# Pre-norm transformer block, one core: attention bursts of one key tile for four quads of heads, 512 columns wide, from the third tile on

## The chip, the cores and the metric

The kernel runs on one core of a Trainium2 chip. The metric is device time in microseconds (us) of one execution. Times come from timed executions and from one profiled execution whose trace names every instruction, its engine, its start and its length.

The engines are TensorE (PE in the profile; its weight loads are PEld), VectorE (DVE), ScalarE (ACT), GpSimd (POOL) and SyncE (SP, which here only issues transfers).

## The reference, cut to what matters

The input x has 2048 rows of 1024 columns; there are 32 heads of 32 columns that share one key head and one value head; the feed-forward part is 3584 wide. Everything is bf16.

```python
def _A_ref(x, wq, wk, wv, wo):          # attention, H = 32, Dh = 32
    q = (x @ wq) as (B, H, S, Dh)
    k = x @ wk; v = x @ wv               # one head for all
    scores = einsum("bhqd,bkd->bhqk", q, k) * Dh ** -0.5
    p = softmax(scores)
    o = einsum("bhqk,bkd->bhqd", p, v)
    return o as (B, S, H * Dh) @ wo
def _B_ref(x, w_gate, w_up, w_down):
    return (sigmoid(x @ w_gate) * (x @ w_up)) @ w_down
h = x + _A_ref(layernorm(x), ...)
out = h + _B_ref(layernorm(h), ...)
```

## The kernel before, in words

**Layout.** `QT` holds the queries transposed: 128 partitions are four heads of 32 dimensions (four strips), 8 slots make 32 heads, 2048 columns are the rows of x. `kT4` holds the transposed keys four times, once per strip. `V` holds the values as 16 key tiles of 128 keys by 32. A tile is 128 rows of x; there are 16 tiles, in 8 units of two.

**Attention.** The work is cut into 64 groups, `ORDER[g] = (t, i)`: tile `t`, and two of the eight slots (eight heads). A group has eight bursts. One burst (`s_burst`, L666 to L680) takes two key tiles: for each key tile four matmuls, one for each strip of 32 partitions, run side by side in TensorE, each 256 columns wide (two slots of 128 rows). They fill two of three pairs of banks in `S_ps`. ScalarE makes two exponentials of 128x1024 from a burst (`one_exp`, L696) and writes them into a ring `Pr` of 18 such tiles, that is, nine bursts. A burst may start when the exponentials of one and a half bursts earlier are out of the banks.

**Values and row sums.** `pv_group` (L759 on) multiplies a group's 16 tiles of exponentials with `V`: four matmuls side by side, one for each strip of 32 output partitions, 256 columns each (L798). For the row sums, VectorE adds the tiles of a group (`add_pair`: L737 adds the two key tiles of a burst, L746 merges the results) into `pairs`, and TensorE multiplies what is left with ones (L777, one or two sets of four matmuls a group, a plan says which) into the right half of the same bank. Groups 0 to 2, group 8 and the very last burst use ones on every tile instead (L795). The bank is evacuated by VectorE: a copy (L816), a 32x32 transposition of the sums (L817), later a reciprocal (L822), a transposition back (L824) and a product (L828) that writes the result over the queries in `QT`.

**Everything else on TensorE.** The projections, wo (both L333), gate and up (L1010) and down (L1080) are groups of full 128x128 matmuls. They and the values share the two banks of `X_ps`; a bank opens again when its evacuation is done.

**Feed-forward part.** A unit's gate and up weights come in "halves" of 256 columns (512 KB, one transfer on SP's queue, L242) into slots that become free: `wgu`, parts of `QT`, and late ones in `Pr` and others. When only the first tile of a unit is ready, `first_tile` runs a pair of halves with 128 columns for that tile alone; the second tile follows as a "later" step. Either the four halves are held for it in their slots, or they are loaded a second time; `may_hold` decides. Down uses 28 matmuls of 512 columns for half a tile.

**Order of the work.** One Python loop writes the order when the kernel is built. It keeps a clock for each engine and issues a burst as soon as its banks should be free, otherwise a piece of the values' group or of the next other group; `dve_fill` puts VectorE's additions into its gaps. The string `PV_PLAN` has a letter for each group that says how its values are started, and a capital says that its sums end in one set of matmuls. On the chip every engine runs its list in this order, held only by semaphores.

Of the kernel before, what the change touches and what calls it, by code (L numbers as in the profile page):

```python
# [7 lines left out]
BF16 = mybir.dt.bfloat16  # L8
# [4 lines left out]
P = 128  # L13
# [71 lines left out]
def bass_sequential_preLN__grouped_kv_mqa__glu_gated_glu__prompt_kernel(  # L85
# [39 lines left out]
    HEAD = ['uuL', 'V', '', '', 'LVLu', 'UU', 'PP', 'LWL', 'zu', 'PPL', 'VV', 'uLPLz', 'PPVL', 'U', 'UPL', 'Pz', 'U', 'UP', 'PzP', 'VV', 'PPU']  # L125
    HEAD_U = [5, 6, 4, 7]
# [12 lines left out]
    with ExitStack() as es:  # L139
        EC = es.enter_context  # L140

        def sb(name, shape, dt=BF16):
            return EC(nc.sbuf_tensor(name, [P] + shape, dt))
# [15 lines left out]
        l8 = sb("l8", [QC // 32], F32)  # L159
# [4 lines left out]
        rs = sb("rs", [2 * NT], F32)  # L164
        vz = sb("vz", [2 * NT])
        sd = sb("sd", [2 * NT])
        powers = sb("powers", [4])
# [70 lines left out]
        def _(unused):  # L238
# [299 lines left out]
            def wq_need(q):  # L538
                return wq_val[q // 2]

            def q_rows(g):
                t, i = ORDER[g]
                return QT[:, 2 * i:2 * i + 2, t * P:(t + 1) * P]

            def q_ready(g):
                t, i = ORDER[g]
                return [q_val[(0, (t, i))]] if t < TPQ else [q_val[(t // TPQ, 2 * i)], q_val[(t // TPQ, 2 * i + 1)]]

            def vq_group(p, qs, on_act=False):
# [70 lines left out]
                return burst(k)[0] * NQ + burst(k)[1]  # L620

            def summed(g):
                return g >= G_SUM and g not in NO_SUM
# [41 lines left out]
            def s_burst(k):  # L665
                g, b = quad(k), burst(k)[2]  # L666
                t, i = ORDER[g]
                mode("s")
                need(pe, (c_e, 2 * k - 1) if k > 0 else None, k_val[b], *q_ready(g), *(xnT_ready(0, 1) if k < 2 else ()))
                for kt in range(2):  # L670
                    for j in range(4):
                        bank = ((2 * k + j // 2) % 3) * 2 + j % 2
                        ins = pe.matmul(S_ps[:, bank, kt * QC:(kt + 1) * QC],  # L673
                                        lhsT=kT4[DH * j:DH * (j + 1), (2 * b + kt) * P:(2 * b + kt + 1) * P],
                                        rhs=QT[DH * j:DH * (j + 1), 2 * i:2 * i + 2, t * P:(t + 1) * P],
                                        start=True, stop=True, tile_position=(DH * j, 0))
                        if kt == 1 and j % 2 == 1:
                            c_s.inc(ins, 0.115, 0.3)
# [42 lines left out]
            def homes(g):  # L721
                return {7: HOME[g % 2][6]} if one_sum(g) else HOME[g % 2]

            def add_pair(k):
                g, b = quad(k), burst(k)[2]
                t, slot, home = (2 * ring(k) + 2) % RP, SLOT[g % 2][b], homes(g)
# [25 lines left out]
                for i, (x, y) in enumerate(steps):  # L752
                    put("p", T_ADD, lambda i=i: merge(i), lambda x=x, y=y: max(when(slot_use[x]), when(slot_use[y])))
# [2 lines left out]
            ot_val = {}  # L756
            ols_read = {}

            def pv_group(g):  # L759
                c = UNIT[ORDER[g][0]]  # L760
                items = []
                is_sum = summed(g)
# [50 lines left out]
                def evac(bank, tick):  # L813
# [5 lines left out]

                    def recip():  # L820
                        need(dve, free)
                        r_ = c_dve.inc(dve.reciprocal(l8[:], ols[:, QC:2 * QC].rearrange("p (a b) -> p a b", b=32)[:, :, 0]), 0.23)  # L822
                        need(dve, r_)
                        t_[0] = c_dve.inc(dve.transpose(ols[:, QC:2 * QC], l8[:].unsqueeze(2).to_broadcast([P, QC // 32, 32])), 0.4)  # L824

                    def mult():
                        need(dve, t_[0])
# [519 lines left out]
            since_s = [0.0]  # L1347
            idle = 0
            while True:
                if wo_val[0] is None and pv_done[0] >= 2 * BPG:  # L1350
                    need(pool, (c_pv, 2 * BPG))
                    wo_val[0] = dma(pool, wo[:], A_wo.rearrange("(q p) n -> p q n", p=P), d_wo, 2048)
# [2 lines left out]
                act_run(k_pe[0])  # L1355
                kk = k[0]
                end = pv_next[0] == NQC * NQ - 1
                pv_ready = pv_next[0] < NQC * NQ and kk >= min(BPG * (pv_next[0] + 1) + 1, NB - end)
                due = when((c_e, 2 * kk - 1))
                plan = PV_PLAN[min(pv_next[0], NQC * NQ - 1)].lower()  # L1360
                late = plan in "ce" and kk == BPG * (pv_next[0] + 1) + 1 and not busy(pv[0])
# [78 lines left out]
                if (pv_next[0] < NQC * NQ and kk > BPG * pv_next[0] + 1 and blocked()  # L1440
                        and UNITS[ffn_list[0][1]][-1] not in hnT_val):
                    pv[0] = pv_group(pv_next[0])
                    pv_next[0] += 1
                    continue
# [37 lines left out]
```

## Time and profile before

| what | us |
|---|---|
| median of 3 timed runs | 1103.26 (1101.07 to 1103.36) |
| the profiled execution | 1102.48 |
| its span, first to last instruction | 1100.7 |
| PE busy | 1075.6, 98% of the span, 15,088 matmuls in the trace |
| PEld busy (weight loads) | 672.5, 61% |
| ACT busy | 1009.7, 92% |
| DVE busy | 885.8, 80% |
| mean DMA rate over the span | 144 GB/s |
| granted TensorE clock, mean | 0.997 |

Busy time is the union of the instructions' lengths. Matmuls overlap with the next one's start, so the pace of TensorE is read from the starts in a timeline, not from their lengths. In the profile, "out<-in" names the tiles an instruction writes and reads, and "<-" behind idle time names what ended it.

### The profile page before, as it was taken

How to read it: one execution, taken by the hardware profiler on the slowest of the kernel's cores; microseconds unless marked ns; L12 is line 12 of the kernel's file. 1: busy time of each engine (PE TensorE's matmuls, PEld its weight loads, DVE VectorE, ACT ScalarE, POOL GpSimd, SP SyncE). 2: the span in 40 equal slices, each digit the busy share in tenths (PEclk: the TensorE clock that was granted, in tenths of full speed). 3: DMA queues.
4: the chain of work that ended last, by engine and by line, in shares of the span. 5: the costliest groups of instructions: out<-in, count | busy, mean ns of one | idle time of the engine just before them, and what ended most of it. 6: DMA issues, size and time to landing. Idle time of an engine off the chain costs nothing. (4 is left out here: it accounts for less than half of the span.)

```text
span 1100.7 us, 34688 instructions
## 1 busy us (share of the span) xinstructions
PE 1075.6 (98%) x15088; PEld 672.5 (61%) x15148; DVE 885.8 (80%) x1586; ACT 1009.7 (92%) x1155; POOL 67.1 (6%) x136
## 2 busy tenths in 40 slices
PE   7999999999999999999999999999999999999999
PEld 5553467654776457664676547764676547764884
DVE  7759968888888888888889888898988888888311
ACT  6999999999999999999999999999999999999110
POOL 4500110100000000000000000000000000000000
PEclk9899999999999999999999999999999999999999
DMA  9852328760675318660585619771495609771760
GB/s 220 141 137 86 106 69 231 223 176 23 158 212 150 91 30 231 174 164 26 153 223 153 145 42 249 197 193 35 120 245 156 153 26 239 201 199 50 163 159 20
DMA packets 299000, 158.88 MB, mean 144 GB/s; under 512 B 39008, under 2 KB 293216, under 8 KB 298848
## 3 DMA queue, kind: packets, MB, share of 16 engines
q1 hardware_dynamic: 293040, 146.43, 51.7%
q0 software_dynamic: 2544, 9.44, 2.6%
q8 instruction: 119, 1.95, 0.8%
q10 hardware_dynamic: 3264, 0.79, 0.4%
q14 instruction: 33, 0.27, 0.1%
HBM read 144.57 MB, written 4.19 MB: 135 GB/s over the span
## 5 line engine op out<-in xcount | busy, mean ns | idle before, releaser
L696 ACT ACTIVATE Pr<-S_ps 128x1024 bf16<-128x1024 f32 x992 | 939.7, 1127 | 4.2 <-PE S_ps L673 3.2
L737 DVE TENSOR_TENSOR pairs<-Pr 128x1024 bf16<-128x1024 bf16 x479 | 324.0, 683 | 51.5 <-ACT Pr L696 48.8
L746 DVE TENSOR_TENSOR pairs<-pairs 128x1024 bf16<-128x1024 bf16 x407 | 280.4, 689 | 25.7 <-DVE pairs L737 1.4
L1010 PE MATMUL X_ps<-QT,wgu 128*128 128x256 bf16 (+1 forms) x2528 | 264.2, 253 | 1.9 <-DMA wgu<-in_B_w_up_dram 1.3
L1010 PEld LDWEIGHTS X_ps<-QT,wgu 128*128 128x128 bf16 x2528 | 198.9, 98 | 51.1 <-issue 30.2
L1080 PE MATMUL X_ps<-zone,hact 128*128 128x512 bf16 (+2 forms) x880 | 206.5, 373 | 6.1 <-issue 5.7
L673 PE MATMUL S_ps<-QT,kT 32*128 32x256 bf16 x4096 | 204.1, 273 | 7.2 <-ACT Pr L696 1.9
L1010 PE MATMUL X_ps<-QT 128*128 128x256 bf16 (+1 forms) x1712 | 172.6, 249 | 0.4 <-DVE ols L817 0.4
L673 PEld LDWEIGHTS S_ps<-QT,kT 32*128 32x128 bf16 x4096 | 61.0, 92 | 151.5 <-ACT Pr L696 128.0
L1010 PEld LDWEIGHTS X_ps<-QT 128*128 128x128 bf16 x1712 | 130.7, 98 | 27.7 <-issue 17.1
L1080 PEld LDWEIGHTS X_ps<-zone,hact 128*128 128x128 bf16 x924 | 79.0, 98 | 99.4 <-issue 24.9
L798 PE MATMUL X_ps<-Pr,V 128*32 128x256 bf16 x3968 | 129.7, 273 | 0.4
L1031 ACT ACTIVATE gu<-X_ps 128x512 f32<-128x512 f32 x112 | 80.4, 718 | 47.5 <-PE X_ps L1010 47.5
L1052 DVE SCALAR_TENSOR_TENSOR hact<-gu,X_ps 128x512 bf16<-128x512 f32 x112 | 76.4, 682 | 47.4 <-PE X_ps L1010 46.9
L798 PEld LDWEIGHTS X_ps<-Pr,V 128*32 128x32 bf16 x3968 | 98.2, 96 | 20.4 <-issue 9.3
L333 PE MATMUL X_ps<-zone 128*128 128x512 bf16 (+3 forms) x576 | 78.7, 281 | 2.7 <-ACT QT L591 1.3
L333 PE MATMUL X_ps<-wo,QT 128*128 128x512 bf16 x240 | 60.6, 380 | 1.6 <-issue 1.1
L333 PEld LDWEIGHTS X_ps<-zone 128*128 128x128 bf16 x576 | 39.5, 100 | 31.9 <-issue 12.9
L348 POOL CAST mean<-mv 128x1 f32<-128x1 bf16 x28 | 8.3, 298 | 818.1 <-DVE mv L923 804.8
L816 DVE COPY ols<-X_ps 128x256 f32<-128x256 f32 x64 | 27.0, 421 | 22.8 <-PE X_ps L777 20.0
L333 PEld LDWEIGHTS X_ps<-wo,QT 128*128 128x128 bf16 x256 | 22.5, 97 | 29.0 <-issue 7.4
L1090 DVE SCALAR_TENSOR_TENSOR hx<-X_ps,hx 128x512 bf16<-128x512 f32 (+2 forms) x33 | 22.1, 670 | 21.7 <-PE X_ps L1080 21.5
(79 smaller groups left out, 449.6 us busy)
## 6 DMA issues: line engine op xcount, KB each, us to landing
wgu<-in_B_w_gate_dram SPq DMA_DIRECT2D x68, 512.0 KB, 5.0
wgu<-in_B_w_up_dram SPq DMA_DIRECT2D x68, 512.0 KB, 5.3
QT<-in_B_w_gate_dram SPq DMA_DIRECT2D x45, 512.0 KB, 5.5
QT<-in_B_w_up_dram SPq DMA_DIRECT2D x45, 512.0 KB, 5.3
zone<-in_B_w_down_dram POOLq DMA_DIRECT2D x14, 512.0 KB, 5.3
out_dram<-hx SPq DMA_DIRECT2D x31, 128.0 KB, 1.7
hx<-in_A_x_dram SPq DMA_DIRECT2D x15, 256.0 KB, 3.2
Pr<-in_B_w_gate_dram SPq DMA_DIRECT2D x5, 512.0 KB, 7.2
```

The source lines that it names most:

```text
L333: ins = pe.matmul(sel(bank), lhsT=a, rhs=b, start=(i == 0), stop=(i == last))
L673: ins = pe.matmul(S_ps[:, bank, kt * QC:(kt + 1) * QC], lhsT=kT4[DH * j:DH * (j + 1), (2 * b + kt) * P:(2 * b + kt + 1) * P], rhs=QT[DH * ...
L696: c_e.inc(act.activation(out=p_tile(k, n % 2), in_=S_ps[:, 2 * pr:2 * pr + 2, :].rearrange("p a (b q) -> p (a b) q", q=QC), func=ACTF.Exp, ...
L737: add_half[k] = slot_use[slot] = c_dve.inc(dve.tensor_tensor(out=pairs[:, slot, :].rearrange("p (j q) -> p j q", j=4), in0=p4[:, :, 0, :], ...
L746: slot_use[x] = slot_use[y] = c_dve.inc(dve.tensor_tensor(out=pairs[:, x, :], in0=pairs[:, x, :], in1=pairs[:, y, :], op=ALU.add), T_ADD, ...
L798: ins = pe.matmul(bank[DH * j:DH * (j + 1), 0:QC], lhsT=V[:, 2 * b + kt, :], rhs=rhs(j), start=first and is_sum, stop=last and plain, tile ...
L816: dve.tensor_copy(out=ols[:, 0:QC], in_=bank[:, 0:QC])
L1010: ins = pe.matmul(bank[:, j * m:(j + 1) * m], lhsT=halves[i][:, dt, j % 2 * P:(j % 2 + 1) * P], rhs=QT[:, dt, r0:r0 + m], start=(dt == 0), ...
L1031: tanh_val[n] = c_act.inc(act.activation(out=slot, in_=bank, func=ACTF.Tanh, scale=0.5), T_TANH, 0.1)
L1052: gu_read[n] = c_dve.inc(dve.scalar_tensor_tensor(out=hact[:, 2 * fs[0]:2 * fs[0] + ft, r0:r0 + len(ts) * P], in0=slot.rearrange("p (a b) ...
L1080: ins = pe.matmul(bank[:, 0:n], lhsT=hact[:, ft, tt * P:(tt + 1) * P], rhs=wd[:, ft, c0:c0 + n], start=(ft == 0), stop=(ft == NFT - 1))
L1090: v = c_dve.inc(dve.scalar_tensor_tensor(out=hv, in0=bank[:, 0:n], scalar=0.5, in1=hv, op0=ALU.mult, op1=ALU.add), 0.03 + n * 0.00113, 0.08)
```

## The change

From group 8 on (the third tile), `wide(g)` holds. Two neighbouring groups of a tile become one block of four slots (16 heads): the first group takes key tiles 0 to 7 of the block, the second key tiles 8 to 15. A burst is one key tile: four matmuls side by side, each 512 columns wide (four slots of 128 rows). It still fills four banks and feeds two exponentials of 128x1024. The values are four matmuls of 512 columns a burst, so that the group fills a whole bank; the first group's bank is copied to a new buffer `olp`, the second's is added to it. The row sums have their own group (`sum_group`) in a bank of its own, once for each block, which the loop starts some bursts after the values (`pv_follow`). VectorE adds the tiles of two neighbouring bursts and merges them into two running tiles for the block. The division is done once a block, on 512 columns.

Beside that, `HR` (tiles of x and h kept) is 4 instead of 5, the two constants `powers` lie in spare columns of `nmean`, `PV_PLAN` is another string, group 8 sums by addition as the others do, the last two bursts use ones directly, and `may_hold` lets units 1 to 3 hold no weights, so that their split steps load them again.

```diff
-    HR = 5
+    HR = 4
-    PV_PLAN = "aadbAdcadEEAEAAAaEEACEAcaEEAECAEaEEECEAAaEEAEEAAaEEAEEAAaEEEeEAa"
+    PV_PLAN = "aaaaAeAaaeaaaeaAaebabaaAdaddaaaAdababaaadabadaaCdabadaaEcaaaacaa"
-    G_SUM, NPB, NO_SUM = 3, 4, (NQ,)
+    G_SUM, NPB = 3, 4
-        ols = sb("ols", [2 * QC], F32)
+        ols = sb("ols", [512], F32)
+        olp = sb("olp", [512], F32)
...
+            def wide(g):
+                return g >= NQ
+            def key_tile(g, b):
+                return ORDER[g][1] % 2 * BPG + b
...
             def direct(k):
-                return k == NB - 1
+                return k >= NB - 2
...
+                if wide(g):
+                    kt = key_tile(g, b)
+                    for j in range(4):
+                        ins = pe.matmul(S_ps[:, ((2 * k + j // 2) % 3) * 2 + j % 2, :],
+                                        lhsT=kT4[DH * j:DH * (j + 1), kt * P:(kt + 1) * P],
+                                        rhs=QT[DH * j:DH * (j + 1), i // 2 * 4:i // 2 * 4 + 4, t * P:(t + 1) * P],
+                                        start=True, stop=True, tile_position=(DH * j, 0))
+                        if j % 2 == 1:
+                            c_s.inc(ins, 0.109, 0.3)
+                    return
...
+            def add_wide(k):
+                g, b = quad(k), burst(k)[2]
+                if b % 2 == 0:
+                    return
...
+                def run(hh):
+                    x = take()
+                    need(dve, (c_e, 2 * k + hh + 1), slot_use[x])
+                    slot_use[x] = c_dve.inc(dve.tensor_tensor(out=dst(x), in0=p_tile(k - 1, hh), in1=p_tile(k, hh), op=ALU.add),
+                                            T_ADD, 0.08)
...
+                def merge(hh):
+                    x, y = run_slot[hh], run_slot[2 + hh]
+                    need(dve, slot_use[x], slot_use[y])
+                    slot_use[x] = slot_use[y] = c_dve.inc(dve.tensor_tensor(
+                        out=pairs[:, x, :], in0=pairs[:, x, :], in1=pairs[:, y, :], op=ALU.add), T_ADD, 0.08)
+                    spare.append(y)
...
+            def pv_wide(g):
...
+                        for j in range(4):
+                            ins = pe.matmul(bank[DH * j:DH * (j + 1), :], lhsT=V[:, kt, :],
+                                            rhs=p_tile(k, j // 2)[:, j % 2 * 2:j % 2 * 2 + 2, :],
+                                            start=b == 0, stop=b == BPG - 1, tile_position=(0, DH * j), skip_group_check=True)
...
+                def evac(bank, tick):
+                    if x % 2 == 0:
+                        force("a", lambda: g - 1 in ols_read)
+                        need(dve, tick, ols_read[g - 1])
+                        olp_val[0] = c_dve.inc(dve.tensor_copy(out=olp[:], in_=bank), 0.62, 0.08)
+                        return olp_val[0]
+                    need(dve, tick, olp_val[0])
+                    olp_val[0] = c_dve.inc(dve.tensor_tensor(out=olp[:], in0=bank, in1=olp[:], op=ALU.add), 0.62, 0.08)
+                    pv_follow[0] = sum_group(g)
+                    return olp_val[0]
...
+            def sum_group(g):
...
+                    for j in range(4):
+                        ins = pe.matmul(bank[DH * j:DH * (j + 1), :], lhsT=ones[:],
+                                        rhs=pairs[:, sum_wide[(g, j // 2)], j % 2 * 512:(j % 2 + 1) * 512],
+                                        start=True, stop=not final, tile_position=(0, DH * j), skip_group_check=True)
...
+                    free = c_dve.inc(dve.transpose(ols[:], bank), 0.75, 0.08)
+                        r_ = c_dve.inc(dve.reciprocal(l8[:], ols[:].rearrange("p (a b) -> p a b", b=32)[:, :, 0]), 0.23)
+                        t_[0] = c_dve.inc(dve.transpose(ols[:], l8[:].unsqueeze(2).to_broadcast([P, 512 // 32, 32])), 0.75)
+                        v = c_dve.inc(dve.tensor_tensor(out=q_rows(g), in0=olp[:].rearrange("p (a b) -> p a b", a=4),
+                                                        in1=ols[:].rearrange("p (a b) -> p a b", a=4), op=ALU.mult), 0.7)
...
-                return c == NU - 1 or n == 0 and c > 0 or c == 0 and n < 2 or 4 * n + 8 <= 4 + c
+                return c == NU - 1 or c == 0 and n < 2 or 4 * n + 8 <= 4 + c
...
+                if not busy(pv[0]) and pv_follow[0] is not None and (
+                        not busy(cur[0]) and not ffn_list or min(bank_time(b) for b in range(2)) <= k_pe[0] + 0.05 and (
+                            PV_PLAN[pv_next[0] - 1].isupper() or k[0] >= NB or
+                            pe_mode[0] == "s" and busy(cur[0]) and cur[0].left() > 0.9 or
+                            k[0] >= BPG * pv_next[0] + 5)):
+                    pv[0], pv_follow[0] = pv_follow[0], None
```

Counted in the two built programs, instruction by instruction (sets are four matmuls side by side):

| on the engines' lists | before | after |
|---|---|---|
| score bursts of 8 matmuls, 256 columns | 512 | 64 |
| score bursts of 4 matmuls, 512 columns | 0 | 448 |
| value sets of 256 / of 512 columns | 1024 / 0 | 128 / 448 |
| ones sets of 256 / of 512 columns | 138 / 0 | 56 / 30 |
| gate and up matmuls of 256 / of 128 columns | 2624 / 1920 | 2368 / 2432 |
| other full matmuls | the same | the same |
| changes between score, value or ones, and full matmuls | 1090 | 1147 |
| VectorE additions of 128x1024 | 886 | 908 |
| VectorE evacuation and division chains of 256 / 512 columns | 64 / 0 | 8 / 28 (and 28 copies) |
| exponentials of 128x1024; tanh | 1024; 112 | 1024; 112 |
| halves of gate and up weights loaded | 240 | 268 |

More of the change, by code (lines that the diff above doesn't have):

```diff
@@ L546, in q_ready @@
                 t, i = ORDER[g]
+                if wide(g):
+                    return [q_val[(t // TPQ, i // 2 * 4 + x)] for x in range(4)]
                 return [q_val[(0, (t, i))]] if t < TPQ else [q_val[(t // TPQ, 2 * i)], q_val[(t // TPQ, 2 * i + 1)]]
@@ L622, in summed @@
             def summed(g):
-                return g >= G_SUM and g not in NO_SUM
+                return g >= G_SUM
             def direct(k):
-                return k == NB - 1
+                return k >= NB - 2
             def burst_no(g, b):
@@ L722, in homes, with unheld, take, dst @@
                 return {7: HOME[g % 2][6]} if one_sum(g) else HOME[g % 2]
+            run_slot, sum_wide, spare = {}, {}, []
+            def unheld():
+                return [x for x in spare if slot_use[x] != "held"]
+            def take():
+                x = min(unheld(), key=lambda x: when(slot_use[x]))
+                spare.remove(x)
+                return x
+            def add_wide(k):
+                g, b = quad(k), burst(k)[2]
+                if b % 2 == 0:
+                    return
+                first, last = key_tile(g, b) == 1, key_tile(g, b) == KT - 1 or direct(k + 2)
+                def dst(x):
+                    return pairs[:, x, :].rearrange("p (a b) -> p a b", b=QC)
+                def run(hh):
[3 more added lines that the diff above has]
+                                            T_ADD, 0.08)
+                    if hh == 1:
+                        add_half[k - 1] = add_half[k] = slot_use[x]
+                    if first:
+                        run_slot[hh] = x
+                    else:
+                        run_slot[2 + hh] = x
+                def merge(hh):
[4 more added lines that the diff above has]
+                    spare.append(y)
+                    if last:
+                        sum_wide[(g, hh)] = x
+                for hh in range(2):
+                    put("p", T_ADD, lambda hh=hh: run(hh), lambda hh=hh: None if not unheld() else
+                        max(when((c_e, 2 * k + hh + 1)), min(when(slot_use[x]) for x in unheld())))
+                    if not first:
+                        put("p", T_ADD, lambda hh=hh: merge(hh), lambda hh=hh: when(slot_use[run_slot[2 + hh]]))
@@ L724, in add_pair @@
             def add_pair(k):
                 g, b = quad(k), burst(k)[2]
+                if wide(g):
+                    if not spare and not run_slot:
+                        spare.extend(range(NPB))
+                    add_wide(k)
+                    return
                 t, slot, home = (2 * ring(k) + 2) % RP, SLOT[g % 2][b], homes(g)
@@ L1357, in _ @@
                 end = pv_next[0] == NQC * NQ - 1
-                pv_ready = pv_next[0] < NQC * NQ and kk >= min(BPG * (pv_next[0] + 1) + 1, NB - end)
+                pv_ready = pv_follow[0] is None and pv_next[0] < NQC * NQ and kk >= min(BPG * (pv_next[0] + 1) + 1, NB - end)
                 due = when((c_e, 2 * kk - 1))
                 plan = PV_PLAN[min(pv_next[0], NQC * NQ - 1)].lower()
-                late = plan in "ce" and kk == BPG * (pv_next[0] + 1) + 1 and not busy(pv[0])
+                late = plan in "ce" and kk == BPG * (pv_next[0] + 1) + 1 and not busy(pv[0]) and pv_follow[0] is None
                 can_s = kk < NB and pv_done[0] >= ring_need(kk - 1 if late else kk)
```

77 lines of the change are left out of this document (71 added, 6 removed).

## The prediction

> **What bounds the kernel now.** I read the busy times first (the page's first part), then the windows of the steady stages, then who waits for whom on TensorE, then a timeline for the pace.
>
> ```profile
> PE 1075.6 (98%) x15088; PEld 672.5 (61%) x15148; DVE 885.8 (80%) x1586; ACT 1009.7 (92%) x1155; POOL 67.1 (6%) x136
> ```
>
> TensorE is nearly full, ScalarE close behind. The windows (length, then busy time of PE, PEld, DVE, ACT, POOL, then clock, DMA share and GB/s) show whether one share hides several stages.
>
> ```profile
> 742.00:867.00 125.00, 123.81 (x1782) 77.00 (x1783) 108.97 (x192) 125.00 (x144) 3.77 (x7) 1.00 0.59 154
> 867.00:991.00 124.00, 122.79 (x1769) 76.84 (x1775) 107.56 (x189) 123.91 (x143) 3.60 (x7) 1.00 0.58 153
> ...
> 1016.00:1101.00 85.00, 82.41 (x835) 62.93 (x836) 18.74 (x33) 8.36 (x14) 1.29 (x3) 1.00 0.49 115
> ```
>
> A unit takes some 124 us, with VectorE at 87%. After the last burst (1013) TensorE works alone for 85 us. The waits on PE's own row between 60 and 1010 us are:
>
> ```profile
> PE X_ps L1080 <- issue: 5.4, 34, 0.2
> PE X_ps L1010 <- DMA wgu<-in_B_w_up_dram: 1.3, 1, 1.3
> PE X_ps L333 <- issue: 1.1, 7, 0.2
> PE X_ps L1010 <- ACT gu L1031: 0.6, 1, 0.6
> PE S_ps L673 <- ACT Pr L696: 0.4, 1, 0.4
> PE X_ps L1010 <- DVE ols L817: 0.4, 1, 0.4
> ```
>
> Leaving "issue" aside (mostly a matmul whose record is missing), TensorE waits about 3 us in 950. So TensorE bounds the kernel: wherever ScalarE is not ready, the order has other matmuls. The time is the sum of what TensorE issues, plus its waits, and only a shorter sum makes it shorter. The pace comes from timelines (start, length, engine, line):
>
> ```profile
> 601.01 0.38 PE L1010 MATMUL X_ps<-QT 128*128 128x256 bf16 x2
> ...
> 601.32 0.40 PE L673 MATMUL S_ps<-QT,kT 32*128 32x256 bf16 x8
> 601.65 1.42 PEld L1010 LDWEIGHTS X_ps<-QT 128*128 128x128 bf16 x14 [0.21 <-issue]
> 601.65 1.70 PE L1010 MATMUL X_ps<-QT 128*128 128x256 bf16 x14
> ```
>
> ```profile
> 538.25 1.07 PE L1010 MATMUL X_ps<-QT 128*128 128x128 bf16 x16
> ```
>
> ```profile
> 1011.56 1.68 PE L1080 MATMUL X_ps<-zone,hact 128*128 128x512 bf16 x7
> ...
> 1013.50 1.71 PE L798 MATMUL X_ps<-Pr,V 128*32 128x256 bf16 x56
> ```
>
> A run's length less the last matmul's own (273, 219, 380 ns in the groups by shape), over the starts between, gives start to start: 256 columns (1.70 - 0.273) / 13 = 0.110 us; 128 columns (1.07 - 0.219) / 15 = 0.057 (most single ones 0.056); 512 columns (1.68 - 0.380) / 6 = 0.217 (most 0.216); a set of four value matmuls (1.71 - 0.28) / 13 = 0.110. Four side by side cost what one costs. A burst takes 0.33 from its start to the next work: 0.120 to the second set's start, 0.010 within it, 0.109 of streaming, and 0.09 for changing between the tiled and the full array. On the way in, the last full matmul starts at 601.01 + 0.38 - 0.273 = 601.12 and the burst 0.205 later: 0.109 streaming, 0.096 change. I take 0.093 for a change.
>
> **The change part by part,** with the counts of the two programs from the table above.
>
> (1) Scores. No trace shows four matmuls of 512 columns side by side. Ends: two sets of 256 as now (0.240 with the start offsets), or one full matmul of 512 (0.216 plus 0.010 of offsets). Sets of 256 pace like one matmul of 256, so I take the near end, 0.227. 448 bursts save 0.0135 each: -6.0 us; 0 is the other end.
>
> (2) Values. 56 groups of 16 sets at 0.1095 become 448 sets at 0.2165: -1.1 us; the ends are 0 and, should the 0.120 that some sets show go too, -2.
>
> (3) Row sums. 138 sets at 0.1095 are 15.1 us; 56 at 0.1095 and 30 at 0.2165 are 12.6: -2.5 us.
>
> (4) Split steps. 512 more matmuls of 128 columns (0.056) and 256 fewer of 256 (0.1093): +0.7 us.
>
> (5) Array changes. The sum has a place of its own, and more value groups are cut by a burst: 1147 for 1090, at 0.093: +5.3 us. This takes back most of (1).
>
> (6) VectorE. 22 more additions at 0.686 (L737 683 ns, L746 689) are +15.1 us. A chain of 256 columns costs 421 + 440 + 197 + 446 + 424 = 1928 ns; 512 columns out of PSUM cost 683 to 690 (L593, L888), 265 more than 256, and so a block of 512 with its second evacuation about 690 + 690 + 710 + 205 + 715 + 690 = 3700 against 3856 for two groups: -4 us. Net +11 us, some 1.5 a unit: 87% becomes 88 to 89%. What hides it is VectorE's idle time, 15 us a unit; if that were gone it would be paid whole. I count 0 on the path.
>
> (7) Banks. With the paces above, I laid out TensorE's work between a bank's last use and its next opening. In before the shortest is 0.86 us and 30 of them are under 1.2, and the rows above show 0.4 us of waiting for an evacuation. After, 48 are under 1.2 and two under the 0.70 that a copy or a transposition of 512 takes (0.31, 0.63). Those two lack 0.5 us; I add 0.3 for the crowd between 0.8 and 1.2: +0.8.
>
> (8) Weights. 28 more halves of 512 KB are 14.7 MB; the eight of a unit add 4.2 MB in 124 us, 34 GB/s on the 153 of the window above. SP issues each in 0.37 us and idles in between for the slots; its transposes and the output queue behind them. A half lands in a median of 5.0 to 5.5 us; the loads stand two to five bursts (4 to 10 us) ahead of their step, as in before's first unit. Bounds: 0 if all are early; 7 added steps at the 1.5 us that the one late half cost at 540.6 would be +10. I take one more late half's worth less the 1.3 of the present one: +0.4.
>
> (9) Tail and start. From the last sum to wo stand 8 down matmuls and 32 of 128 columns, 1.73 + 1.8 = 3.5 us, over a chain of 0.7 + 0.2 + 0.7 + 0.7 = 2.3: hidden. Between wo and the second tile's first use, tile 14's remaining 160 matmuls of 128 take 9.0 us, over about 7 (in before, wo ends at 1023.9 and the second tile's transpose is issued at 1027.6 and lands 3.3 later): hidden, with 2 us to spare. `HR`, `powers` and the first 41 us: the order there is the same, 0; their cover is that tile t - 4 is long written out when tile t is wanted. ScalarE issues the same list.
>
> Sum: -6.0 - 1.1 - 2.5 + 0.7 + 5.3 = -3.6 of TensorE's work, +1.2 of waits: -2.4. On the profiled 1102.48 that is 1100.1; the median of the three runs is 0.8 above the profiled one, so I give the middle, 1100.4.
>
> **The rivals.**
>
> *A, nothing measurable* (within 0.2%, 2.2 us, about what a measurement of this kernel can tell from no change). The 18 additional openings under 1.2 us and the tight weights give back 2 to 4: 1101 to 1104. For it: the waits now are 3 us in all, so they can hardly fall. Against: before's 30 such openings cost 0.4.
>
> *B, VectorE becomes the bound; slower.* The place is the evacuation behind one addition that has just begun (0.69 us): an opening with less than 0.86 + 0.69 = 1.55 us of cover then waits. After, 76 openings lack 30 us in total against that; before, 69 lack 21. It decides from about a fifth of the 30 on, 6 us; at a third it is 10 - 3.6, or 1109. Against: before paid next to nothing of its 21.
>
> *C, the second loads come late; slower.* A split step of four halves needs 7 us of transfers at the 290 GB/s of the best 10 us, and it lasts two or three bursts, 4 to 6 us. Units 3 and 6 have two or three in a row. At (8)'s upper end, 1102.5 - 3.6 + 10 = 1109. Against: the queue holds them bursts ahead.
>
> *D, more gain.* The waits go too (3 us), or the value sets lose more: 1096 to 1097.
>
> *E, the cost of a matmul is per instruction.* 3,584 score and value matmuls fewer, and if each cost but a tenth of a set of 256 (0.011), -39 us: 1063. Against: 0.110 for four side by side leaves 0.003 beyond the columns. The Trainium skill ("TensorEngine Tiling (Array Packing)", section Instruction Overhead) says that each matmul has about 60 cycles of overhead; by that, and 2.4 GHz, an estimate is 3,584 x 25 ns = 90 us, or 22 us where four overlap. The trace does not bear it out at these widths: two sets of 256 take 0.219 and one matmul of 512 takes 0.216.
>
> **How the numbers follow.** The forecast (1097.5 to 1101) 0.48; A 0.22; B 0.13; C 0.10; D 0.06; E 0.01. The range 1096 to 1108 leaves out E, and B and C beyond their middle. Faster by over 0.2%: forecast without its edge, D and E, 0.52; within: A and that edge, 0.25; slower: B and C, 0.23.
>
> **What would show it.** After: TensorE's row of waits below 6 us between 60 and 1010; a 512-column burst of 0.317 us from its start to the next work; the last burst some 2 us earlier; the stage behind it 1 to 2 us shorter; VectorE busy near 897. Wrong would be: four side by side at 512 slower than 0.24, waits on `olp`, `ols` or `pairs` on TensorE's rows (B), waits on `wgu` or `QT` transfers (C).

## The result and the profile after

| | before | after |
|---|---|---|
| median of 20 runs each, us | 1102.53 (1101.07 to 1103.83) | 1100.26 (1098.54 to 1102.60) |
| ratio, 95% interval | | 0.9978 [0.9971, 0.9985] |
| the profiled execution, us | 1102.48 | 1100.95 |
| its span, us | 1100.7 | 1098.9 |

The changed kernel is faster by 0.22%, some 2.3 us. The forecast of 1100.4 is met within 0.2 us. The terms that it was added up from are not: two of them were wrong by 4.7 and 5.5 us in opposite directions, and this is what the rest of the document is about.

First the busy times, the first part of the page of the kernel after (engine, busy us, share of the span, instructions):

```profile
PE 1082.9 (99%) x11612; PEld 616.4 (56%) x11612; DVE 899.6 (82%) x1496; ACT 1008.4 (92%) x1155; POOL 64.5 (6%) x136
```

Some 3,500 matmul records fewer, and 56 us fewer of weight loads, are seen here beside a time that is only 0.2% shorter. Weight loads lie beside the matmuls, so their share says nothing about the pace here. VectorE is at 899.6 us where 897 was forecast.

The windows of the same stages (length, then busy time of PE, PEld, DVE, ACT, POOL, clock, DMA share, GB/s), after:

```profile
742.00:867.00 125.00, 124.37 (x1253) 68.41 (x1250) 110.40 (x176) 124.72 (x144) 3.12 (x7) 1.00 0.58 153
867.00:991.00 124.00, 123.50 (x1306) 68.95 (x1304) 107.17 (x172) 123.65 (x142) 3.79 (x7) 1.00 0.67 171
1016.00:1101.00 85.00, 80.84 (x824) 61.91 (x820) 19.82 (x32) 8.37 (x14) 1.29 (x3) 0.99 0.43 113
```

VectorE's 110.40 of 125 us is the 88% that the prediction gave. TensorE is still full in both steady stages. ScalarE's row is as full (124.72 of 125), but a busy row is not a row without room: in the trace its exponentials start 0.904 us apart where nothing holds them up (the five at 767.97 in the timeline below are such a row), and the next instruction starts 0.48 us behind the start of a tanh. For the 974 exponentials and 98 tanh from burst 25 to the last burst this makes an estimate of 927 us, in a stretch of 944 (946 before). So ScalarE has some 18 us of room there, and the reading that TensorE's list of work bounds the kernel holds; the run with added changes of the array, below, puts it to the test.

The waits on PE's own row between 60 and 1010 us, after (waiting line, what it waited for, us in all, times, longest). The view has no further lines:

```profile
PE X_ps L1180 <- issue: 1.1, 2, 0.6
PE X_ps L334 <- DVE V L586: 0.3, 1, 0.3
PE S_ps L695 <- ACT Pr L718: 0.2, 1, 0.2
```

No row names a weight transfer: rival C (second loads) did not come, and before's single wait of 1.3 us for a transfer is gone too. No row names `olp`, `ols` or `pairs` either, but the row "issue" hides two waits for an evacuation. A timeline of all engines at these two places:

```profile
767.97 4.69 ACT L718 ACTIVATE Pr<-S_ps 128x1024 bf16<-128x1024 f32 x5 [0.28 <-issue]
...
769.87 0.69 DVE L856 TENSOR_TENSOR olp<-X_ps,olp 128x512 f32<-128x512 f32 x1 [0.16 <-PE X_ps L842]
...
770.66 0.33 PE L1180 MATMUL X_ps<-QT,wgu 128*128 128x128 bf16 x3 [0.63 <-issue]
```

```profile
894.39 0.68 DVE L856 TENSOR_TENSOR olp<-X_ps,olp 128x512 f32<-128x512 f32 x1
...
895.18 0.77 PE L1180 MATMUL X_ps<-QT 128*128 128x128 bf16 x11 [0.50 <-issue]
```

Both times a group of full matmuls starts 0.10 us behind the end of L856, the evacuation of a block's values (769.87 + 0.69 = 770.56, and 895.07). It does so at the same two places in the runs below with values, scores or both cut and with 56 additions. Against the usual pace the two cost 0.70 and 0.57 us. These fit the two openings with too little work before them that term (7) counted. Rival B, an evacuation that stands behind an addition, is hardly in them: the first began as soon as its bank was full, the second some 0.2 us later.

Last the pace, a timeline on PE, after (start, length, engine, line, tiles, count):

```profile
616.51 0.40 PE L685 MATMUL S_ps<-QT,kT 32*128 32x512 bf16 x4
616.84 1.68 PE L1250 MATMUL X_ps<-zone,hact 128*128 128x512 bf16 x7
618.46 0.40 PE L685 MATMUL S_ps<-QT,kT 32*128 32x512 bf16 x4
618.78 0.40 PE L881 MATMUL X_ps<-pairs,ones 128*32 128x512 bf16 x4
619.11 1.25 PE L1250 MATMUL X_ps<-zone,hact 128*128 128x512 bf16 x5
```

From a burst's start to the next full matmul are 616.84 - 616.51 = 0.33 us. That is what a burst took before the change. The mean over all 448 is 0.327 (0.325 where values follow), where the prediction had 0.317; a burst of eight matmuls of 256 columns has 0.330 (0.327). Everything that follows starts from this line.

**The account.** From the trace I took the stretch from the start of burst 25, where the loop's steady part begins, to the start of the last matmul. I priced TensorE's list in it with the paces seen in the traces, and call what is left the excess: waits, and some 7 to 8 us of small differences that every kernel here has.

| us | before | after | difference |
|---|---|---|---|
| stretch from burst 25 to the last matmul | 1031.1 | 1028.0 | -3.1 |
| list of work in it | 1017.5 | 1018.7 | +1.2 |
| excess | 13.7 | 9.3 | -4.3 |
| of it, gaps that can be named | 5.7 | 2.1 | -3.6 |
| burst 25 starts at | 67.2 | 68.6 | +1.4 |

Each figure is rounded for itself. Of the list, streaming is 912.2 and 908.1 us, and 1029 and 1086 changes of the array at 0.0955 are 98.3 and 103.7; the rest is about 7 in each. Each column is one profiled execution, but other executions bear them out: the kernel before with `HR` = 4, whose order is before's, has a stretch of 1031.2, and the kernels with the changed order and narrower sets have an excess of 8.6 (scores cut), 10.2 (values) and 11.1 (both).

So TensorE has slightly more to do after the change, not 3.6 us less; and it waits less, not more.

### The profile page after: what moved, and what is told of

Read it like the earlier page. It is cut to its first block, busy times and chain, and to the rows that moved or that the text cites. A ratio compares the mean times of both kernels' runs of the same rounds, so it can differ in the third digit from the quotient of the medians.

```text
span 1098.9 us, 27392 instructions
## 1 busy us (share of the span) xinstructions
PE 1082.9 (99%) x11612; PEld 616.4 (56%) x11612; DVE 899.6 (82%) x1496; ACT 1008.4 (92%) x1155; POOL 64.5 (6%) x136
## 4 chain that ended last, share of the span: by engine, by line
PE 95%; ACT 2%; DVE 1%; DMA 1%; POOL 1%; issue 0%; DVEq 0%; ACTq 0%
PE X_ps L1180 38%; PE X_ps L1250 19%; PE S_ps L685 13%; PE X_ps L334 10%; PE X_ps L842 10%; PE S_ps L695 1%; PE X_ps L968 1%; ACT Pr L718 1%; PE X_ps L881 1%; DVE st L381 1%; PE X_ps L965 1%; ACT hact L718 1%; DMA zone<-zone 0%; DMA hx<-in_A_x_dram 0%; POOL sd L360 0%
## 5 line engine op out<-in xcount | busy, mean ns | idle before, releaser
L768 DVE TENSOR_TENSOR pairs<-Pr 128x1024 bf16<-128x1024 bf16 x446 | 303.6, 683 | 28.4 <-ACT Pr L718 27.7
L780 DVE TENSOR_TENSOR pairs<-pairs 128x1024 bf16<-128x1024 bf16 x390 | 268.9, 689 | 11.0
L1180 PE MATMUL X_ps<-QT,wgu 128*128 128x128 bf16 (+1 forms) x2656 | 257.7, 247 | 0.7 <-issue 0.6
L1250 PE MATMUL X_ps<-zone,hact 128*128 128x512 bf16 (+2 forms) x924 | 216.9, 374 | 0.0
L685 PE MATMUL S_ps<-QT,kT 32*128 32x512 bf16 x1792 | 176.8, 385 | 0.0
L1180 PE MATMUL X_ps<-QT 128*128 128x128 bf16 (+1 forms) x1840 | 175.8, 245 | 0.6 <-issue 0.5
L685 PEld LDWEIGHTS S_ps<-QT,kT 32*128 32x128 bf16 x1792 | 45.1, 91 | 129.9 <-ACT Pr L718 114.3
L842 PE MATMUL X_ps<-Pr,V 128*32 128x512 bf16 x1792 | 114.7, 381 | 0.0
L842 PEld LDWEIGHTS X_ps<-Pr,V 128*32 128x32 bf16 x1792 | 40.2, 96 | 50.8 <-issue 16.8
L334 PEld LDWEIGHTS X_ps<-zone 128*128 128x128 bf16 x576 | 39.3, 99 | 33.5 <-issue 13.9
L903 DVE STREAM_TRANSPOSE ols<-X_ps 128x512 f32<-128x512 f32 x28 | 20.0, 716 | 23.0 <-PE X_ps L881 21.5
```

Of the source, the lines that this page charges most:

```text
L334: ins = pe.matmul(sel(bank), lhsT=a, rhs=b, start=(i == 0), stop=(i == last))
L685: ins = pe.matmul(S_ps[:, ((2 * k + j // 2) % 3) * 2 + j % 2, :], lhsT=kT4[DH * j:DH * (j + 1), kt * P:(kt + 1) * P], rhs=QT[DH * j:DH * ( ...
L768: slot_use[x] = c_dve.inc(dve.tensor_tensor(out=dst(x), in0=p_tile(k - 1, hh), in1=p_tile(k, hh), op=ALU.add), T_ADD, 0.08)
L780: slot_use[x] = slot_use[y] = c_dve.inc(dve.tensor_tensor(out=pairs[:, x, :], in0=pairs[:, x, :], in1=pairs[:, y, :], op=ALU.add), T_ADD, ...
L842: ins = pe.matmul(bank[DH * j:DH * (j + 1), :], lhsT=V[:, kt, :], rhs=p_tile(k, j // 2)[:, j % 2 * 2:j % 2 * 2 + 2, :], start=b == 0, stop ...
L903: free = c_dve.inc(dve.transpose(ols[:], bank), 0.75, 0.08)
```

## The experiments

**Is it the width? Values in halves.** The changed kernel with each set of value matmuls cut into two of 256 columns; order and all else as it is.

```diff
-                        for j in range(4):
-                            ins = pe.matmul(bank[DH * j:DH * (j + 1), :], lhsT=V[:, kt, :],
-                                            rhs=p_tile(k, j // 2)[:, j % 2 * 2:j % 2 * 2 + 2, :],
...
+                        for h in range(2):
+                            for j in range(4):
+                                ins = pe.matmul(bank[DH * j:DH * (j + 1), h * QC:(h + 1) * QC], lhsT=V[:, kt, :],
+                                                rhs=p_tile(k, j // 2)[:, j % 2 * 2 + h, :],
...
```

> The changed kernel with its 448 value sets of 512 columns cut into 896 sets of 256 (1,792 more matmuls, all else the same). Theory S (TensorE pays for columns and for changes of the array, not for instructions): 448 x (0.219 - 0.2165) = +1.1 us on the changed kernel, a ratio to before of about 0.999 against the 0.998 of the changed kernel. Rival E (a fixed cost for each matmul): 1,792 x 0.011 = +20 us, ratio 1.016; if four side by side share it, +5 us, ratio 1.002.

Measured: 1101.35 us, 0.9991 [0.9981, 1.0001] to before, so 0.0013 or 1.4 us above the changed kernel, with intervals that overlap. Its list is 1.2 us longer. A line of the timeline of this run:

```profile
624.88 1.38 PE L843 MATMUL X_ps<-Pr,V 128*32 128x256 bf16 x44
```

44 matmuls are 11 sets: (1.38 - 0.28) / 10 = 0.110 us a set, as before the change. 1,792 more matmuls cost 1.4 us, and rival E, a price per instruction, had at least 5. By the Trainium skill ("TensorEngine Tiling (Array Packing)", section Instruction Overhead), with its 60 cycles for each matmul, 25 ns as in the prediction's estimate, an estimate would have been 1,792 x 25 ns = 45 us; the run does not agree.

**Scores in halves.** The same cut for the 448 wide bursts, values left wide.

```diff
-                    for j in range(4):
-                        ins = pe.matmul(S_ps[:, ((2 * k + j // 2) % 3) * 2 + j % 2, :],
+                    for h in range(2):
+                        for j in range(4):
+                            ins = pe.matmul(S_ps[:, ((2 * k + j // 2) % 3) * 2 + j % 2, h * QC:(h + 1) * QC],
...
-                        if j % 2 == 1:
+                            if h == 1 and j % 2 == 1:
```

> The changed kernel with each of its 448 score bursts of four matmuls of 512 columns cut into two sets of 256 in the same banks (1,792 more matmuls, all else the same). Theory S: 448 x 0.0135 = +6.0 us (0.011 by the paces alone: +4.9), ratio about 1.003; a burst takes 0.330 us from its start to the next work instead of 0.317. Rival E: +20 us, ratio 1.016. Rival that the offset between the two sets is hidden: ratio 0.998 as for the changed kernel.

Measured: 1100.24 us, 0.9981 [0.9972, 0.9989]: with the cut the ratio is the same within 0.0003, where the intervals are 0.0008 wide to each side. The 6 us, or 0.0054, that term (1) gave to the width of the scores are not there. The timeline of this run:

```profile
614.95 0.40 PE L686 MATMUL S_ps<-QT,kT 32*128 32x256 bf16 x8
615.28 1.68 PE L1251 MATMUL X_ps<-zone,hact 128*128 128x512 bf16 x7
```

Eight matmuls of 256 columns take 0.33 us to the next work (0.330 in the mean), four of 512 take 0.327. Why the prediction had 0.317: in a burst of 256 the first set takes 0.120, not 0.1095, to the second set's start. I took those 10 ns for a price of the second set, which one wide set would not pay. From the last score matmul's start to the next full matmul it is 0.200 us at 256 columns and 0.317 at 512, so 0.117 more and not 0.107: the wide set pays the same 10 ns behind a change of the array, only at another place. Full matmuls pay it too: behind a burst the first one takes 0.226 us to the next where 0.216 is usual at 512 columns, and 0.120 for 0.109 at 256.

**Both cut.** If the gain is the width alone, this kernel must have before's time.

> The changed kernel with score bursts and value sets both cut into sets of 256 columns, in the same order, blocks and banks: all that is left of the change is the order, the blocks of four quads with their sums, and the rule for weights. Bursts in the trace of the changed kernel take 0.327 us where the cut ones took 0.330, so scores are worth 448 x 0.003 = 1.3 us and values 448 x 0.0025 = 1.1. Theory S2 (width is worth 2.4 us, and that is the whole gain): ratio 1.000. Theory O (the order has fewer waits and that is the gain): 0.9985 or less.

Measured: 1103.21 us, 1.0000 [0.9991, 1.0009]. The two cuts alone cost 0.0013 and 0.0003, and together 0.0022, or 2.4 us (the interval allows 1 us to each side), which is the whole gain of the change. In the account its list is 1021.1 us, 2.4 above the changed kernel's and 3.5 above before's, and its excess is 11.1 against 13.7 before. So all that is not width (additions, chains, plan, split steps, array changes) comes out at nothing, within that 1 us: it costs some 3 to 4 us of list and saves some 3 of waits. The waits of this run on PE's row, 60 to 1010 us:

```profile
PE X_ps L1183 <- DMA wgu<-in_B_w_up_dram: 1.4, 2, 0.9
PE X_ps L1183 <- issue: 1.1, 2, 0.6
PE X_ps L1183 <- DMA wgu<-in_B_w_gate_dram: 0.5, 1, 0.5
```

Waits of rival C's kind, for weight transfers, stand here, 1.9 us, though the order is that of the changed kernel, in which the row had none. The loads lie at the edge: they can be late or not in the same order.

**Weights held as before.** The changed kernel with before's rule for units 1 to 3, so that their split steps keep their four halves.

```diff
-                return c == NU - 1 or c == 0 and n < 2 or 4 * n + 8 <= 4 + c
+                return c == NU - 1 or n == 0 and c > 0 or c == 0 and n < 2 or 4 * n + 8 <= 4 + c
```

> The changed kernel with the rule for held weights of before (units 1 to 3 hold one pair again; 232 halves loaded instead of 268, 10,972 matmuls instead of 11,612). Theory S: TensorE's list sums to 1.4 us less (1.7 less in split steps, 3 more changes of the array), ratio about 0.9965, if nothing waits. Rival W (held slots make the other halves late): waits for transfers on TensorE's rows, 1.5 us each, two or three of them: ratio 0.998 to 1.001.

Measured: 1112.69 us, 1.0090 [1.0077, 1.0103], slower than the changed kernel by 12 us. The list is 1.3 us shorter (1017.4), and the excess is 22.6 against 9.3. The first wait on PE's row, and the timeline at the start of a unit:

```profile
PE S_ps L685 <- ACT Pr L718: 8.0, 9, 1.9
```

```profile
417.09 0.39 PE L685 MATMUL S_ps<-QT,kT 32*128 32x512 bf16 x4 [0.33 <-ACT Pr L718]
419.41 0.39 PE L685 MATMUL S_ps<-QT,kT 32*128 32x512 bf16 x4 [1.93 <-ACT Pr L718]
419.74 0.68 PE L1180 MATMUL X_ps<-QT,wgu 128*128 128x128 bf16 x9
421.24 0.61 PE L685 MATMUL S_ps<-QT,kT 32*128 32x512 bf16 x4 [0.83 <-ACT Pr L718]
```

Between 417.09 and 419.41 the order has nothing but bursts, and TensorE waits for ScalarE's exponentials. That the four slots that are held leave no weights for another step is how I read it; no run shows it by itself. The work that found no place there is done behind the last burst: up to it the kernel takes 946.2 us from burst 25 (944.4 in the changed kernel), but behind it stand 48 more matmuls of 512 columns, 10.4 us, and that stage is 93.8 us instead of 83.6. Both theories missed: one said faster, the other named transfers as what TensorE waits for.

**The new rule in the kernel before.** The same edit the other way round.

```diff
-                return c == NU - 1 or n == 0 and c > 0 or c == 0 and n < 2 or 4 * n + 8 <= 4 + c
+                return c == NU - 1 or c == 0 and n < 2 or 4 * n + 8 <= 4 + c
```

> The kernel before with the changed rule for held weights alone (units 1 to 3 hold none and load again; narrow bursts, plan and HR as before). From the 25th burst on TensorE's list sums to 1017.3 us against 1017.5 of before (1018.7 of the changed kernel), and the chip took 13.7 us more than the sum in before, 9.3 in the changed kernel. Theory R (the rule took the waits away, whatever the width): the excess falls to about 9, ratio 0.996. Theory J (rule and width belong together; the narrow kernel had no place where the rule helps): the excess stays at 13 to 15, ratio 0.999 to 1.002.

Measured: 1112.59 us, 1.0083 [1.0069, 1.0097]. No theory had this. The list is the same as before's within 0.2 us (1017.3), the excess 22.7 against 13.7. PE's row of waits, the first four:

```profile
PE S_ps L673 <- ACT Pr L696: 3.9, 5, 1.9
PE X_ps L1010 <- DVE ols L817: 2.3, 3, 0.9
PE X_ps L798 <- ACT gu L1031: 1.7, 2, 1.0
PE X_ps L1010 <- ACT gu L1031: 1.6, 1, 1.6
```

Each rule is some 10 us worse in the other kernel. `PV_PLAN` has a letter for each group, and each kernel's string stands beside its own rule. I take it that the two are fitted to each other; no run with a string fitted to the other rule shows it. Only the first row here is a wait for ScalarE's exponentials; the others are banks that open late. So neither run gives the rule's own price, only that of the rule in an order of the other kernel.

**One letter of the plan for nearly all groups.** The changed kernel with "d" for groups 8 to 62, which starts value groups so that they are cut less often by bursts.

```diff
-    PV_PLAN = "aaaaAeAaaeaaaeaAaebabaaAdaddaaaAdababaaadabadaaCdabadaaEcaaaacaa"
+    PV_PLAN = "aaaaAeAaddddddddddddddddddddddddddddddddddddddddddddddddddddddda"
```

> The changed kernel with the letter d in the plan for all wide groups but the last: values are not interrupted by a burst. The built order has 1,113 changes of the array instead of 1,147, and TensorE's list sums to 2.8 us less from the 25th burst on. Theory S (TensorE's list decides): 2 to 3 us faster than the changed kernel, ratio to before about 0.9955. Rival P (value groups in one piece make bursts late, ScalarE runs dry, and the work behind the last burst grows or TensorE waits): ratio 0.998 or more.

Measured: 1110.60 us, 1.0061 [1.0047, 1.0075], 9 us above the changed kernel. By the same prices the list is 2.7 us shorter (1016.0), but the excess rose from 9.3 to 20.9. PE's row of waits, the first two:

```profile
PE S_ps L685 <- ACT Pr L718: 5.0, 8, 0.9
PE X_ps L1180 <- DMA QT<-in_B_w_gate_dram: 1.3, 2, 0.9
```

The order with fewer changes of the array loses more than four times as much in waits as it saves in its list.

**What a change of the array costs.** The changed kernel with one matmul of 32 columns, tiled and without use, ahead of 257 groups of full matmuls: 514 more changes of the array in the same order (`main[0]` is set where the main loop starts). It only adds work.

```diff
...
+                    if g.kind == "f" and pe_mode[0] == "f" and main[0]:
+                        pe.matmul(X_ps[0:DH, g.bank, 0:DH], lhsT=ones[:], rhs=ones[:], start=True, stop=True,
+                                  tile_position=(0, 0), skip_group_check=True)
...
```

> The changed kernel with one tiled matmul of 32 columns put in front of 257 groups of full matmuls that follow a full matmul (it writes into the group's own bank, which the group's first matmul overwrites): 514 more changes of the array, nothing else moved. Theory S: 257 x (0.093 + 0.0955 + 0.025) = +55 us, ratio to before 1.048. Rival (a change that follows the end of a group is hidden in part): +27 us or less, ratio 1.022.

Measured: 1157.96 us, 1.0493 [1.0479, 1.0508]; that is 0.0515 x 1103.5 = 56.8 us above the changed kernel, 0.22 us a pair. The matmul itself streams for 0.025 us (the pace of the 32-column matmuls at the kernel's start), so a change there and back costs 0.19 to 0.20. A timeline of this run:

```profile
612.31 0.82 PE L1184 MATMUL X_ps<-QT 128*128 128x256 bf16 x6
613.06 0.19 PE L312 MATMUL X_ps<-ones 128*32 128x32 bf16 x1
613.18 0.62 PE L1184 MATMUL X_ps<-QT,wgu 128*128 128x128 bf16 x8
```

The last matmul ahead starts at 612.31 + 0.82 - 0.273 = 612.86, so it is 0.20 us from there to the tiled one (0.109 streaming, 0.09 the change), and 0.12 on to the next full one. The price adds up in full, so TensorE and not ScalarE, whose list is the same, sets the time: at 0.0955 each, the 57 more changes of the changed kernel are the 5.4 us in its list. The Trainium skill ("TensorEngine Tiling (Array Packing)", section Key Properties) says that changing the tiling mode drains TensorE and gives no figure; here a change costs time, as a drain would, but no run shows that it is the drain.

**How much room VectorE has.** The changed kernel with 112 additions made a second time: 77 us more for VectorE by the length of one (0.69 us), 64.5 us more in its busy time (964.1).

```diff
+                    if hh == 0 and b in (3, 7):
+                        extra = c_dve.inc(dve.tensor_tensor(out=dst(x), in0=p_tile(k - 1, hh), in1=p_tile(k, hh), op=ALU.add))
+                        extra[0].wait(dve, extra[1])
```

> The changed kernel with 112 additions of 128x1024 on VectorE done twice (a repeat into the same tile; order of everything else the same): +112 x 0.686 = 77 us of VectorE's time in the 950 us of attention, from 88% to about 96%. Theory F (VectorE's idle time hides it): TensorE's waits grow by less than 3 us, ratio 0.998 to 1.001. Rival B (evacuations behind an addition decide): at least a fifth to a third of the 30 us that the tight openings lack, +6 to +10 us and more, ratio 1.004 to 1.01.

Measured: 1125.38 us, 1.0198 [1.0184, 1.0212], 24 us above the changed kernel. PE's row of waits, the first three:

```profile
PE X_ps L884 <- DVE olp L859: 3.8, 8, 0.8
PE X_ps L884 <- DVE hx L1263: 2.9, 4, 1.0
PE X_ps L1253 <- DVE olp L859: 2.5, 3, 1.3
```

These are rival B's waits: a bank of `X_ps` opens late because its evacuation stands behind an addition. The theory that so much is hidden falls. Whether the change's own additions already pay is not answered by so large a dose, so I halved it.

**Half as much.** 56 additions made again (`b in (3,)` in the edit above): 38 us by length, 30.9 in the busy time (930.5).

> As the run with 112 repeated additions on VectorE, with 56: +38 us of VectorE's time. There 77 us cost 25 us of waits on TensorE. If the cost is in proportion (0.32 us for each us): +12 us, ratio 1.009, and the 11 us that the change adds to VectorE cost some 3. If it only begins beyond some share (idle time hides the first part): +4 us or less, ratio 1.002 or less, and the 11 us cost next to nothing.

Measured: 1105.60 us, 1.0020 [1.0011, 1.0029], 4.6 us above the changed kernel; the excess rises by as much (13.9). A cost in proportion would have been 12; this is near the 4 of the theory that the cost only begins beyond some share. The first 56 additions cost 4.6 us and the next 56 cost 20. VectorE is busy for 818.5 of the 950 us from 60 to 1010 before, 832.6 after, 858.1 here and 872.2 with 112. The curve bends upwards, so the change's own 13.8 us of busy time (899.6 - 885.8) cost at most, by an estimate along the straight line, 13.8 x 4.6 / 30.9 = 2.1 us; of the changed kernel's two waits for an evacuation, only some 0.2 us lie behind an addition.

**The start.** Burst 25 starts 1.4 us later after the change. The kernel before with one thing of the change that reaches into the start:

```diff
-    HR = 5
+    HR = 4
```

> The kernel before with HR = 4 alone. In the changed kernel the tenth burst starts 1.4 us later than in before, behind a transposing transfer. Theory H (the fifth tile of x now lands in another buffer and meets other transfers): burst 10 again 1.4 us later, ratio 1.001. Rival L (chance in when a transfer lands): burst 10 where it is in before, ratio 1.000. Later stages: no wait for hx, since tile t - 4 is long written out: no difference from 60 us on.

Measured: 1102.44 us, 1.0002 [0.9993, 1.0011]; burst 25 at 66.85 us against 67.2. `HR` costs nothing. In the other runs of the changed kernel, all with the same order up to there, burst 25 starts anywhere from 65.9 to 69.6 us. Each is one profiled execution. The 1.4 us lie within what they differ in this part.

## Why the prediction was right, and where it was not

The direction, the size and the bound that carries them were right: TensorE's list of work decides. VectorE stayed beside the path but for the two openings of 1.3 us, and the second loads of weights cost nothing that the trace shows. That the sum came out so near is luck: term by term, in us, from burst 25 on, it was not right.

| step of the prediction | forecast | found | from |
|---|---|---|---|
| (1) scores | -6.0 | -1.3 | account; the run with the scores cut agrees within its noise |
| (2), (3) values and row sums | -3.6 | -3.6 | account |
| (4) split steps | +0.7 | +0.7 | account |
| (5) array changes | +5.3 | +5.4 | account; 257 added pairs cost 0.22 each |
| sum of the list | -3.6 | +1.2 | |
| (6) VectorE, (7) banks, (8) weights: waits | +1.2 | -4.3 | account |
| (9) behind the last burst | 0 beyond the list | -1.5 in all | 85.2 to 83.6 us, forecast 1 to 2 shorter |
| start, to burst 25 | 0 | +1.4 | one profiled execution; chance |

**Term (1) is the step that failed.** "Sets of 256 pace like one matmul of 256, so I take the near end, 0.227" was the choice; the other end, 0.240 or nothing saved, was nearly right (0.237 by the trace). The rows for it were in the profile of before, but they were read wrongly: 0.120 instead of 0.1095 behind a change of the array is not a price of having two sets. It is paid by whatever comes first behind the change. The run with scores cut in half shows it best, since 6 us should have come back, and 0.3 us did (0.0003), which is within the noise.

**The waits are the second one, with the wrong sign.** (7) and (8) added 1.2 us to 3 us of waits. (7)'s two tight openings did come, at 1.3 us for the 0.8 forecast. But all else fell: the gaps that can be named went from 5.7 to 2.1, most of all by the one late half of weights (1.5 us). Rival D, the one in which the waits go too, had this part right, at a chance of 0.06, and rival A's sentence that the waits "can hardly fall" is wrong: waits in PE's own row were 3 us, but the gaps in the trace add up to 5.7, in a stretch of 13.7 us over its list, so there was more to gain than the row shows.

So the total is right by two errors that cancel: +4.7 in the list, -5.5 in the waits. And the gain of 0.15 to 0.29% (the interval) reaches into rival A's 0.2%, so the runs hardly tell the two apart by the time. Of the five signs that the prediction named, three came (the row of waits below 6 us, the stage behind the last burst 1.5 us shorter, VectorE near 897) and two did not (a burst of 0.317 us; the last burst 2 us earlier, which is only 0.2 earlier, at 1012.98, since this execution started 1.4 later).

VectorE's division chain (6) was sized rightly, as the groups by shape of the kernel after show (busy us, mean ns):

```profile
L853 DVE COPY olp<-X_ps 128x512 f32<-128x512 f32 x28 | 19.3, 688 | 3.1 <-PE X_ps L842 2.7
L856 DVE TENSOR_TENSOR olp<-X_ps,olp 128x512 f32<-128x512 f32 x28 | 19.3, 688 | 6.4 <-PE X_ps L842 6.0
...
L903 DVE STREAM_TRANSPOSE ols<-X_ps 128x512 f32<-128x512 f32 x28 | 20.0, 716 | 23.0 <-PE X_ps L881 21.5 <-PE X_ps L894 1.0
```

With the reciprocal (247), the second transposition (711) and the product (691) a block is 688 + 688 + 716 + 247 + 711 + 691 = 3741 ns for a forecast of 3700.

**What the change is, then.** The width alone is worth 2.4 us by the run with both cut, give or take 1 us; by the paces, 1.3 of it is the scores' and 1.1 the values'. The rest of the change comes out at nothing: more changes of the array against shorter waits. Why the changed order waits less is not settled. The rule put back alone made the excess 22.6, and another plan string (not before's) made it 20.9, so it goes with rule and string together. With the width put back it was 11.1, which is little more than what executions with this order differ by (8.6 to 10.2 with one of the two cuts). No run separates what is the order's from what is luck of the fit. A plan string fitted to each rule was not run, so whether holding the weights is worse in itself stays open.

## What to carry to other kernels

Where TensorE's list is the bound, price the whole list, each change between a tiled and a full array included (0.19 to 0.20 us there and back here), and do not count on width: four matmuls side by side at 512 columns instead of two sets at 256 save 3 ns, because the columns set the pace. A small premium seen on "the first of two" must be looked up behind a change and elsewhere before it is counted as saved. Where an order is written out ahead, changing one part of what it is made from moved the waits by some 10 us here, more than the parts are worth; compare parts by cutting instructions in the same order, and check each term, because a right total may hide two wrong ones. And where a row of waits says "issue", look at what ended just before on the other engines: here it was an evacuation.

## What the runs showed of the hardware that was not expected

- What comes first behind a change of the array is some 10 ns longer: a tiled set at 256 columns (0.120 against 0.1095 to the next set) and at 512 (0.317 to the next full matmul, where the 0.200 at 256 columns and 0.107 more streaming would make 0.307), and a full matmul (0.226 against 0.216 at 512).
- A change between two tiled shapes costs as much as one to the full array: from a burst's start (32 x 128) to the next values (128 x 32) it is 0.325 us, to the next full matmul 0.327.
- Load on VectorE costs little and then much: 56 additions of 0.69 us more cost 4.6 us of time, the next 56 cost 20, with VectorE busy for 90.3% and 91.8% of the stretch from 60 to 1010 us (858.1 and 872.2 of 950).
- The first 68 us of profiled executions with the same order there differ by up to 3.7 us (burst 25 at 65.9 to 69.6).
